# Finished head pairs normalised on GpSimd, a deeper evacuation queue and all-VectorE rungs in the last units

## The chip, the cores and the metric

The kernel runs on one core of a Trainium2 chip. The metric is the device time of one execution in microseconds. The engines named here are TensorE (PE in the profile, PEld for its weight loads), VectorE (DVE), ScalarE (ACT), GpSimd (POOL) and the DMA queues of SyncE (SP) and GpSimd. PSUM is the memory that TensorE writes its results to; SBUF is the working memory.

## The reference

Two attention layers over 2048 tokens, 512 channels and 32 heads of 16 channels run side by side, and their outputs are joined along the channels. Cut to what matters:

```
A (4 segments of 512 tokens, M and z carried from segment to segment):
  q, k, v = x@wq, x@wk, x@wv                 per head
  a_dot = softmax(q k^T * 16**-0.5, causal inside the segment) v
  a_mem = (phi(q) M) / (phi(q) z + 1e-6);  phi(t) = t+1 if t>0 else exp(t)
  o = g * a_mem + (1-g) * a_dot;           g = sigmoid(beta) per head
  M += phi(k)^T v ;  z += sum phi(k) ;     result  o @ wo
B (all 2048 tokens, no mask):
  o = softmax(q k^T * 16**-0.5) v ;        result  o @ wo
```

B's score matrices are the bulk: 32 heads of 2048 x 2048, each entry of which has to go through an exponential.

## The kernel before

**Units.** The work is cut into units. One unit holds four heads of one group of eight (the heads of one parity, `e`, of a row tile `rt`) for 512 queries. Two units, e = 0 and e = 1, make a pair. A has 16 pairs (four segments of four), B 16 pairs (four query blocks `ch` of four). The order is: A's four pairs of segment 0, then B and A pairs in turn until A's twelve others are used up, then B's last four pairs alone. A unit of B meets 16 key blocks of 128 keys; a pair of A is only five such blocks' worth, because of the mask.

**Two ways to exponentiate a key block.** On the first way, TensorE writes the scores of a key block (four heads, four banks of 512) into PSUM tiles `s_ps` of three and two banks in turn, and ScalarE exponentiates a tile at a time into `pT` (L906). For A, GpSimd then clears what the mask excludes (`affine_select`, L916). On the second way, which only B's key blocks can take, TensorE writes each head's scores into a one-bank tile `v_ps`, and VectorE turns them into 16-bit integers `vx` whose bits, read as float16, are an approximate exponential (L979, four evacuations a key block). Three more copies of that tile are made with other offsets from `LADDER`, so that the errors of the four average out. These copies are called rungs here. Two are made by VectorE (L993). The third is made in place by a DMA that adds a constant tile `fill` to `vx` once the first tile has been used (`v_sum`, L1000, issued from GpSimd's queue). All four are multiplied by the values, so a block on the second way costs TensorE four products with the values instead of one.

**Accumulators and pairs.** Products with the values go into a one-bank PSUM tile `acc` per unit. Three such one-bank slots exist, and `acc`, `v_ps`, the projections' results, A's memory products `am_ps` and the output projections all share them. When a unit is done, VectorE transposes `acc` into one half of an SBUF tile `tT` (L378, `fin_unit`). There is one `tT` only: `held["tT"]` is set when the first unit of a pair is transposed, and cleared when the pair is finished (`pair_end`). The next pair's first transpose has to wait for that. `fin_pair` (L396) then finishes the pair: a reciprocal of the softmax sums (L401), for A more small reciprocals, then the normalisation. For B and A's segment 0 that is one multiplication (L412); for A's later segments it is two multiplications and an addition (L420, L422, L424). Last comes a transpose into the output tile `OT` (L426). B's very last pair takes another way, `fin_half`.

**The planner.** The order of instructions on every engine is written out when the program is built, by a model of the engines' clocks (`T["pe"]`, `T["dve"]`, `T["pool"]` and so on). VectorE's work waits in a list of tasks and is put into the program when the model's VectorE gets to it; lower `prio` goes first, so evacuations (0) come before a pair's steps (1), and these before rungs (2). The first score tile of a key block for VectorE is issued only while `backlog()`, the model's VectorE work in hand, is below `VBACK` microseconds, and a one-bank slot is free (`v_scores`, L959). `v_pick` (L934) takes the key block: from the current unit or one of the next, at most three blocks ahead of the current unit, none when a unit has about three left (these go to ScalarE), and none before unit 8. So how many key blocks VectorE takes is not fixed; it follows from how early the model thinks VectorE is free.

**The way to GpSimd that is there already.** In `fin_pair` the normalising instructions ask for an engine by `yield (POOLTT, ...)`. `in_turn` (L741) gives GpSimd only if `T["pool"] < T["pe"] + POOLSLACK` and fewer than two such requests wait. With `POOLSLACK = -99` this is never so, and the instruction goes to VectorE. If it were so, `pool_run` (L1006) would hold the request until VectorE has at least `POOLWITH` = 1.2 microseconds of work queued that does not share SBUF's ports with GpSimd by the model (evacuations from PSUM; tasks marked `port` are the others), or until `POOLWAIT` = 4 microseconds have gone by. The model gives it `POOLTT` = 1.2 microseconds, and both sides keep clear of each other's `port` stretches (`clear`, `begin`, `on_pool`).

Of the kernel before, what the change touches and what calls it, by code (L numbers as in the profile page):

```python
# [37 lines left out]
LADDER = (12914, 13046, 13325, 13628)  # L38
# [1 line left out]
VBUFS = 12  # L40
VMIN = 3
VLATE = 0.5
VBACK = 1.0
BANKS = (3, 2)
PBUFS = 8
SWITCH = 0.095
# [12 lines left out]
DMARUNG = 3  # L59
# [4 lines left out]
SPLOADS = 38.0  # L64
SPTRANS = 1.5
POOLTT = 1.2
POOLSLACK = -99.0
POOLWITH = 1.2
POOLWAIT = 4.0
LEAD = 2.5  # L70
# [7 lines left out]
def kernel(  # L78
# [21 lines left out]
    def pin(ins):  # L100
        return tc.keep_in_program_order(ins)
# [42 lines left out]
    def later(us, f, src=None, prio=0, ready=None, ok=None, port=False):  # L144
        if not live[0]:
            f()
            return
        if ready is None:
            ready = T["pe"] + PELAT
        seq[0] += 1  # L150
        tasks.append(dict(prio=prio, seq=seq[0], ready=ready, us=us, f=f, src=src, ok=ok, port=port))
# [319 lines left out]
    with ExitStack() as ms:  # L471
# [51 lines left out]
        units, pos0, where = [], {}, 0.0  # L523
# [212 lines left out]
        def backlog():  # L736
            return max(0.0, T["dve"] - T["pe"]) + sum(t["us"] for t in runnable() if t["ready"] < T["pe"] + 0.6)
# [3 lines left out]
        def in_turn(g, prio, end=None):  # L741
            on = [None]

            def step():
# [7 lines left out]
                if isinstance(c, tuple):  # L752
                    if T["pool"] < T["pe"] + POOLSLACK and len(ptasks) < 2:
                        on[0] = nc.gpsimd
# [22 lines left out]
        def free_slots(at):  # L777
            return sum(s <= at for s in slots)
# [155 lines left out]
        def v_pick():  # L934
            if vnow[0] is not None:
                return True
            if vlive[0] > VBUFS - 2:
                return False
            vmin = VMIN + VLATE * (max(0.0, T["dve"] - T["pe"]) + sum(t["us"] for t in tasks)) / QUAD
            for i in range(u_at[0], min(u_at[0] + 5, len(units))):  # L940
                u = units[i]
                if u["name"] == "a" or len(u["kbs"]) < vmin:
                    continue
                kb = u["kbs"][-1]
                if i > cur[0] and vahead[0] >= VAHEAD or not has(u, kb) or i < VFROM:
                    return False
                u["kbs"].pop()
                u["left"] += len(LADDER)
                u["nv"] = u.get("nv", 0) + 1
                vlive[0] += 1  # L950
                vahead[0] += i > cur[0]
                x = wk.tile([P, 4, 512], U16, name="vx", tag="vx", bufs=VBUFS)
                vnow[0] = (u, kb, x, list(q4))
                return True
            return False
# [3 lines left out]
        def v_scores(taken, lim=2, force=False):  # L959

            n = 0
            while n < lim and (force or backlog() < VBACK) and free_slots(T["pe"] + (0.1 if taken else 0.0)) and v_pick():
                u, kb, x, left = vnow[0]
# [13 lines left out]
        def v_evac(u, kb, x, j, vt, end):  # L977
            def f():
                pin(nc.vector.tensor_scalar(x[:, j, :], vt[:], XSCALE, float(LADDER[0]), ALU.mult, ALU.add))  # L979
                if end:  # L980
                    buf = [len(LADDER) - 1, u, kb, x]
                    v_ready(u, kb, x, buf)
                    for i in range(1, len(LADDER)):
                        if i != DMARUNG:
                            later(0.70, v_rung(u, kb, x, LADDER[i], buf), prio=2, ready=T["dve"],
                                  ok=lambda: vlive[0] < VBUFS, port=True)
            return f

        def v_rung(u, kb, x, off, buf):
            def f():  # L990
                vlive[0] += 1
                p = wk.tile([P, 4, 512], U16, name="vx", tag="vx", bufs=VBUFS)
                pin(nc.vector.tensor_scalar(p[:], x[:], float(off - LADDER[0]), 32767.0, ALU.add, ALU.min))  # L993
                v_ready(u, kb, p, [1])
                v_done(buf)
            return f
# [22 lines left out]
        def v_ready(u, kb, p, buf, at=None):  # L1019
            pd = p[:].bitcast(F16)  # L1020
            pvq.append(dict(u=u, kb=kb, v=buf, ready=(T["dve"] + DVEEND if at is None else at) + 0.06,
                            parts=[(pd, j, j, (u, kb, 0, 512, 0), None) for j in q4]))
# [408 lines left out]
```

## Time and profile before

| what | value |
|---|---|
| median of three runs | 884.29 us (883.23 to 884.37) |
| the profiled execution's own time | 883.22 us |
| its span, first to last instruction | 881.5 us |
| busy: PE, ACT, DVE, POOL | 853.3, 854.8, 755.7, 269.6 us |
| ACT's exponentials, L906 | 736 instructions, 843.4 us |
| DVE's score evacuations, L979 | 528 (132 key blocks), 345.9 us |
| DVE's rungs, L993 | 264, 173.5 us |
| DMA rungs, L1000 | 132, 512 KB each, 4.9 us to landing |
| normalisations on DVE, L412, L420, L422, L424 | 19, 12, 12, 12 |
| granted TensorE clock | 0.998 |

A row of the table of groups gives the line, the engine and operation, the tile written and the tile read, shapes, the number of instructions, their busy time together, the mean of one in nanoseconds and, after the bar, the time for which the engine was idle just before them with what ended most of it. Instructions in a row on one engine overlap a little, so busy time over count is less than the mean. A stretch of the span, where one is shown, lists each engine's busy time in it. A time line gives the start, the duration, the engine and line, and in brackets the idle time before it.

### The profile page before, as it was taken

To read this page: it belongs to the slowest core of one execution; us is meant where nothing else is said; L and a number is where in the kernel's file an instruction comes from. 1 tells how busy PE (TensorE), PEld (TensorE's weight loads), DVE (VectorE), ACT (ScalarE), POOL (GpSimd) and SP (SyncE) were. 2 spreads that over 40 slices of the span, in tenths; PEclk is the share of its full clock that TensorE was granted. 3 is DMA by queue.
4 is the path that set the end of the run, shared out by engine and by line. 5 is a ranking of instruction groups with operands and counts; after the bars stand their busy time and mean duration, and the time that the engine had idled before them with its cause. 6 is when DMAs were issued, how large, how long until landed. Compare 5 with 4: busy or idle time off the path is not lost.

```text
span 881.5 us, 19327 instructions
## 1 busy us (share of the span) xinstructions
PE 853.3 (97%) x7725; PEld 253.6 (29%) x7725; DVE 755.7 (86%) x1280; ACT 854.8 (97%) x766; POOL 269.6 (31%) x466
## 2 busy tenths in 40 slices
PE   8999999999999999999999999999999999999995
PEld 3322222322323222222232223223232322222221
DVE  4778499889898888979989999888979899999994
ACT  6999999999999999999999999999999999999994
POOL 6711402433424134241331414215241411212111
PEclk9999999999999999999999999999999999999999
DMA  9404315345164554533547463554636355756754
GB/s 197 91 14 101 91 29 96 79 88 97 31 120 90 116 114 80 96 76 69 103 78 135 99 135 73 97 97 94 122 62 116 77 126 103 134 107 130 144 112 101
DMA packets 61811, 86.28 MB, mean 98 GB/s; under 512 B 36624, under 2 KB 44816, under 8 KB 61712
## 3 DMA queue, kind: packets, MB, share of 16 engines
q0 software_dynamic: 19008, 69.21, 41.7%
q1 hardware_dynamic: 41360, 15.23, 7.5%
q8 instruction: 62, 1.02, 0.5%
q10 hardware_dynamic: 1344, 0.52, 0.2%
q14 instruction: 37, 0.30, 0.1%
HBM read 4.20 MB, written 4.19 MB: 10 GB/s over the span
## 4 chain that ended last, share of the span: by engine, by line
PE 34%; ACT 15%; issue 7%; DVE 3%; DMA 1%; POOL 1%; ACTq 0%; POOLq 0%; DVEq 0%
PE acc L121 18%; ACT pT L906 15%; PE s_ps L121 9%; PE v_ps L121 5%; DVE vx L979 1%; DMA vx<-fill 1%; POOL pT L916 1%; DVE vx L993 1%; PE o_ps L121 1%; PE q_ps L121 0%; PE am_ps L121 0%; ACT ex L303 0%; DVE tT L378 0%; PE k_ps L121 0%; PE m_ps L121 0%
## 5 line engine op out<-in xcount | busy, mean ns | idle before, releaser
L906 ACT ACTIVATE pT<-s_ps 128x1536 bf16<-128x1536 f32 x736 | 843.4, 1284 | 8.6 <-PE s_ps L121 4.9
L979 DVE TENSOR_SCALAR vx<-v_ps 128x512 uint16<-128x512 f32 x528 | 345.9, 685 | 43.4 <-PE v_ps L121 34.4
L121 PE MATMUL s_ps<-qB,KB 32*128 32x512 bf16 x1520 | 245.3, 383 | 10.0 <-ACT pT L906 7.2
L1000 POOL DMA_DIRECT2D vx<-fill x132 | 115.9, 890 | 452.7 <-PE v_ps L121 132.2
L121 PE MATMUL v_ps<-qB,KB 32*128 32x512 bf16 x528 | 188.3, 381 | 1.0 <-DVE vx L979 0.5
L121 PE MATMUL acc<-vx,VB 128*32 128x512 f16 x2112 | 185.2, 384 | 2.8 <-DMA vx<-fill 1.1
L993 DVE TENSOR_SCALAR vx<-vx 128x2048 uint16<-128x2048 uint16 x264 | 173.5, 690 | 2.6
L121 PEld LDWEIGHTS <-KB 32*128 32x128 bf16 x2048 | 82.5, 91 | 249.5 <-issue 244.1
L121 PE MATMUL acc<-pT,VB 128*32 128x512 bf16 x1520 | 147.2, 386 | 0.0
L916 POOL TENSOR_SCALAR_AFFINE_SELECT pT<-pT 128x256 bf16<-128x256 bf16 (+2 forms) x242 | 102.6, 455 | 68.9 <-ACT pT L906 67.9
L121 PE MATMUL acc<-zeros 128*128 128x512 bf16 x369 | 123.3, 386 | 0.0
L121 PEld LDWEIGHTS <-VB 128*32 128x32 bf16 x3632 | 74.6, 94 | 164.7 <-issue 149.6
L121 PE MATMUL s_ps<-qA,kA 32*128 32x512 bf16 (+3 forms) x512 | 53.1, 300 | 2.8 <-ACT pT L906 1.5
L378 DVE STREAM_TRANSPOSE tT<-acc 128x512 f32<-128x512 f32 x64 | 44.5, 700 | 12.7 <-PE acc L121 12.7
L121 PEld LDWEIGHTS <-zeros 128*128 128x128 bf16 x385 | 31.0, 97 | 71.6 <-issue 64.8
L278 POOL TENSOR_SCALAR qA<-qc,par 128x512 bf16<-128x512 bf16 x24 | 18.4, 775 | 59.9 <-DVE qc L276 59.9
L121 PE MATMUL acc<-pT,vA 128*32 128x256 bf16 (+3 forms) x512 | 31.6, 305 | 1.2 <-DVE vA L323 0.5
L276 DVE CAST qc<-q_ps 128x512 bf16<-128x512 f32 x28 | 19.2, 685 | 10.4 <-PE q_ps L121 9.6
L121 PEld LDWEIGHTS <-kA 32*128 32x128 bf16 x512 | 16.9, 92 | 38.4 <-issue 36.1
L278 POOL TENSOR_SCALAR qB<-qc,par 128x512 bf16<-128x512 bf16 x32 | 23.3, 746 | 9.4 <-DVE qc L276 9.4
L458 DVE CAST osb<-o_ps 128x512 bf16<-128x512 f32 x28 | 19.2, 687 | 6.7 <-PE o_ps L121 6.7
L121 PE MATMUL o_ps<-wo_a,OT_a 128*128 128x512 bf16 x64 | 19.8, 384 | 0.0
(93 smaller groups left out, 432.2 us busy)
## 6 DMA issues: line engine op xcount, KB each, us to landing
vx<-fill POOLq DMA_DIRECT2D x132, 512.0 KB, 4.9
out_dram<-osb SPq DMA_DIRECT2D x30, 128.0 KB, 1.7
w_b<-in_B_wqkv_dram SPq DMA_DIRECT2D x3, 512.0 KB, 5.8
phk<-phkT SPq DMA_TRANSPOSE x48, 2.4
w_a<-in_A_wv_dram SPq DMA_DIRECT2D x1, 512.0 KB, 4.3
wo_a<-in_A_wo_dram SPq DMA_DIRECT2D x1, 512.0 KB, 4.7
wo_b<-in_B_wo_dram SPq DMA_DIRECT2D x1, 512.0 KB, 8.1
xT_b<-in_B_x_dram SPq DMA_TRANSPOSE x28, 2.9
```

The source lines that it names most:

```text
L121: return pin(nc.tensor.matmul(out, lhsT, rhs, **k))
L276: pin(nc.vector.tensor_copy(qc[:], ps[:]))
L278: pin(nc.gpsimd.tensor_scalar(dst[:, e, :], qc[:], par[:, e:e + 1], 0.0, ALU.mult, ALU.add))
L378: pin(nc.vector.transpose(st["tT"][:, e].rearrange("p c d -> p (c d)"), acc[:]))
L458: pin(nc.vector.tensor_copy(osb[:], ps[:]))
L906: pin(nc.scalar.activation(pT[:, 0:n, :], pt[:, 0:n, :], ACT.Exp, scale=SCALE))
L916: pin(nc.gpsimd.affine_select(out=blk, in_=blk, compare_op=ALU.is_ge, fill=0.0, base=0, pattern=[[0, len(sls)], [1, P]], channel_multiplie ...
L979: pin(nc.vector.tensor_scalar(x[:, j, :], vt[:], XSCALE, float(LADDER[0]), ALU.mult, ALU.add))
L993: pin(nc.vector.tensor_scalar(p[:], x[:], float(off - LADDER[0]), 32767.0, ALU.add, ALU.min))
L1000: pin(nc.gpsimd.dma_start(out=x[:].rearrange("p j c -> p (j c)").rearrange("p (a c) -> p a c", c=FILL), in_=fill[:].to_broadcast([P, 2048 ...
```

## The change

Three things are changed, all in what the planner decides.

1. `POOLSLACK` goes from -99 to 1.0. The normalising multiplications and additions of finished pairs may now go to GpSimd, under the conditions given above. Whether each one does depends on the model at that moment.
2. `VBACK` goes from 1.0 to 1.5. Score tiles for VectorE are issued while the model has up to 1.5 microseconds of VectorE work in hand.
3. In the last two units (B's last pair) the third rung is no longer made by the DMA: `buf` gets the count of all four rungs and no tile for `v_sum`, and the loop makes one more `v_rung` task, a VectorE pass of L993's kind into a buffer of its own.

```diff
-VBACK = 1.0
+VBACK = 1.5
...
-POOLSLACK = -99.0
+POOLSLACK = 1.0
...
                 if end:
                     buf = [len(LADDER) - 1, u, kb, x]
+                    if u["id"] >= len(units) - 2:
+                        buf = [len(LADDER)]
                     v_ready(u, kb, x, buf)
                     for i in range(1, len(LADDER)):
-                        if i != DMARUNG:
+                        if i != DMARUNG or u["id"] >= len(units) - 2:
                             later(0.70, v_rung(u, kb, x, LADDER[i], buf), prio=2, ready=T["dve"],
                                   ok=lambda: vlive[0] < VBUFS, port=True)
```

## The prediction

> **What bounds the kernel now.** I read the page's busy times and groups first, then three stretches of the span, then VectorE's own waits, then two pieces of the time line: a hand-over between pairs and the end. From the table of groups:
>
> ```profile
> L906 ACT ACTIVATE pT<-s_ps 128x1536 bf16<-128x1536 f32 x736 | 843.4, 1284 | 8.6 <-PE s_ps L121 4.9
> L979 DVE TENSOR_SCALAR vx<-v_ps 128x512 uint16<-128x512 f32 x528 | 345.9, 685 | 43.4 <-PE v_ps L121 34.4
> L1000 POOL DMA_DIRECT2D vx<-fill x132 | 115.9, 890 | 452.7 <-PE v_ps L121 132.2
> L121 PE MATMUL acc<-zeros 128*128 128x512 bf16 x369 | 123.3, 386 | 0.0
> L993 DVE TENSOR_SCALAR vx<-vx 128x2048 uint16<-128x2048 uint16 x264 | 173.5, 690 | 2.6
> ```
>
> And the stretches with A mixed in, and with B alone (us, then busy time of PE, PEld, DVE, ACT, POOL):
>
> ```profile
> 45.00:705.00 660.00, 646.21 (x5830) 191.72 (x5832) 573.71 (x975) 654.57 (x588) 204.39 (x343) 1.00 0.46 89
> 705.00:865.00 160.00, 157.06 (x1511) 45.04 (x1503) 150.88 (x248) 158.67 (x140) 31.36 (x36) 1.00 0.64 123
> ```
>
> ScalarE is busy for 99% of both, and its exponentials wait 8.6 us in all. It is the bound. TensorE looks as full, but 369 of its matrix products multiply zeros into an accumulator: filler that gives way. So the time is ScalarE's count of key blocks, and it falls only if VectorE takes more of them. VectorE idles 660 - 573.7 = 86 us in the mixed stretch, 9 us in B's own.
>
> **The exchange rate.** A key block is four banks of L906's 1840 (736 tiles of 2.5): 4 x 843.4/1840 = 1.83 us of ScalarE. On VectorE it is 4 x 345.9/528 + 2 x 173.5/264 = 2.62 + 1.31 = 3.93 us. A block that moves shortens the span by 1.83 us, and VectorE, kept at its present share of 0.86, loses 0.86 x 1.83 = 1.57 us of room. It therefore takes 5.50 us of VectorE time to move one block, and a freed microsecond of VectorE is worth 1.83/5.50 = one third of a microsecond. TensorE pays three more groups of products a block, 0.22 us apart in the time line of the end: 0.65 us, out of the filler's 123 us.
>
> **Part 1, normalisation on GpSimd.** The rows, each shape apart:
>
> ```profile
> L412 DVE TENSOR_TENSOR tN<-tT,rsum 128x512 bf16<-128x512 f32 x15 | 10.5, 703 | 0.1
> L424 DVE TENSOR_TENSOR tN<-tT,aT 128x512 bf16<-128x512 f32 x12 | 8.6, 715 | 0.4
> L422 DVE TENSOR_TENSOR aT<-aT,r 128x512 f32<-128x512 f32 x12 | 8.2, 680 | 0.0
> L420 DVE TENSOR_TENSOR tT<-tT,r 128x512 f32<-128x512 f32 x12 | 7.7, 646 | 0.0
> L278 POOL TENSOR_SCALAR qB<-qc,par 128x512 bf16<-128x512 bf16 x32 | 23.3, 746 | 9.4 <-DVE qc L276 9.4
> ```
>
> That is 35.0 us in 51 instructions. (The four of A's segment 0 come before VectorE takes key blocks, and free nothing.) GpSimd is 31% busy in the mixed stretch, and a request that meets it busy stays on VectorE; I take 47 of 51, 32 us, worth 10.7 us of span. Bounds 28 to 35 us.
>
> What it costs: GpSimd's instruction has no row. The nearest is L278 with one input, 0.68 us alone and up to 1.64 us behind VectorE; I take 1.3 us, bounds 0.7 and 2.4 (L278's mean alone, and that mean on top of its longest). The Trainium skill, GPSIMD Engine Reference, section 4.1 Engine selection, speaks against the move: two-input elementwise work belongs on VectorE, and GpSimd is about twice as slow. By it the instruction would take about 1.4 us, an estimate, and the sum would be the same to 0.2 us.
>
> Queued behind it on GpSimd are mask clears (L916), query splits (L278) and DMA issues (L1000). A delay of 1.3 us there I cost at nothing: the eight `pT` tiles between ScalarE and the products last 8 x 1.15 = 9.2 us. If that cover went, ScalarE would wait for each microsecond beyond it. The output projections behind L426 have due times eight tiles and more later, so SP's stores move with no cost.
>
> Now the wait. The request may be held for up to 4 us, and L426, `held["tT"]` and the next pair's first transpose stand behind it. The time line of VectorE at a hand-over from B to A:
>
> ```profile
> 220.52 0.71 DVE L378 STREAM_TRANSPOSE tT<-acc 128x512 f32<-128x512 f32 x1
> ...
> 225.64 0.68 DVE L412 TENSOR_TENSOR tN<-tT,rsum 128x512 bf16<-128x512 f32 x1
> 226.36 0.71 DVE L426 STREAM_TRANSPOSE OT_b<-tN 128x512 bf16<-128x512 bf16 x1
> 226.99 0.68 DVE L378 STREAM_TRANSPOSE tT<-acc 128x512 f32<-128x512 f32 x1
> ```
>
> A's first transpose starts as soon as B's pair lets go of `tT`: so at 8 of the 12 such hand-overs (the other four have 0.8 to 2.9 us between). Each microsecond of delay keeps one of three PSUM slots from score tiles. I take 2.0 us of holding and 0.6 us of slower instruction at the eight and 1 us at the four: 25 us, of which VectorE loses half, since a third slot and rungs are left to it: 12 us, worth -4.0. Bounds 0 and 12 x (4.0 + 0.5) = 54 us. After A's pairs nothing presses: the next transpose comes 12 to 21 us later.
>
> **Contention.** VectorE and GpSimd hold each other up when both work from SBUF (GpSimd's two query splits, then VectorE's two-input instruction):
>
> ```profile
> 336.05 2.31 POOL L278 TENSOR_SCALAR qB<-qc,par 128x512 bf16<-128x512 bf16 x2 [0.91 <-DVE qc L276]
> ```
>
> ```profile
> 336.25 1.03 DVE L309 SCALAR_TENSOR_TENSOR phq<-ex,po 128x512 bf16<-128x512 f32 x1
> ```
>
> L309 takes 0.69 us undisturbed. L979 beside GpSimd work keeps its 0.685. The worst stretch of a rung is 0.24 us (0.93 against 0.69). I take 0.1 us for each of 47, 4 us rounded, worth -1.3; bounds 0 and 47 x 0.7 = 33 us, a rung that waits out half an instruction each time. The Trainium skill, SBUF — State Buffer, section Who interferes with whom, calls the shared port an exclusive lock: the later one waits for the whole instruction, which the stretched rows here only show in part. By it, if every instruction met a rung, the estimate is 47 x 1.3 = 61 us, -20 instead of -1.3.
>
> **Part 2, the deeper queue.** VectorE's waits:
>
> ```profile
> DVE vx L979 <- PE v_ps L121: 34.4, 91, 1.4
> DVE vx L979 <- PE s_ps L121: 4.1, 12, 0.9
> ```
>
> A mean gap of 0.38 us before an evacuation would be covered by 0.5 us more in hand, if a slot is free, which with three it often is not. Some gaps come from the limit of three blocks ahead, which stays. Bounds 0 and 38 us; I take 15, worth 5.0. The wait it adds is before projections' evacuations in the same queue, 0.5 us at most, again under the 9.2 us of `pT`.
>
> **Part 3, the end.** Time line, all engines:
>
> ```profile
> 865.95 0.86 POOL L1000 DMA_DIRECT2D vx<-fill  x1 [3.08 <-PE acc L121]
> ...
> 869.03 0.39 PE L121 MATMUL acc<-vx,VB 128*32 128x512 f16 x4
> 870.51 0.40 PE L121 MATMUL acc<-vx,VB 128*32 128x512 f16 x4 [1.09 <-DMA vx<-fill]
> ...
> 870.96 0.72 DVE L378 STREAM_TRANSPOSE tT<-acc 128x512 f32<-128x512 f32 x1 [5.54 <-PE acc L121]
> ```
>
> Without the DMA the last product ends at about 869.5, as its neighbours do: 1.4 us gained directly (bounds 0 and 1.5); late next are ScalarE's last tile (its products start at 868.60) and the fixed end after it. The last two units hold ten blocks for VectorE (11 of 16 on ScalarE in each): ten passes of 0.657 us, 6.6 us, of which 1.3 lies in the 5.5 idle us above. 5 us, worth -1.7. Ten DMA issues of 0.88 us leave GpSimd, where nothing waits for them.
>
> **Sum.** 10.7 - 4.0 - 1.3 + 5.0 - 1.7 + 1.4 = 10.1 us off the profiled execution's 883.22 (span 881.5 and 1.7 around it): 873.1. That execution is 1.1 us under the median, so 874.2, rounded to 874.0.
>
> **Rivals.**
> - *The hold at the hand-over eats it* (slower). One mechanism: at the 12 B-to-A hand-overs one slot is left, so 1.2 us of evacuations cannot be queued, the request runs into its 4 us, and all of it is lost. 54 us, -18 instead of -4: 884.3 + 18 - 14.1 = 888. It decides from 4.0 us lost at each (48 us, -16). For it: the eight tight hand-overs; against: rungs, which need no slot.
> - *GpSimd's instruction takes 2.4 us where the plan has 1.2* (slower). VectorE's queue stands at L426 behind it: 51 x 1.2 = 61 us, -20: about 894. For it: two inputs, float, strided; against: L278's 0.68.
> - *Freed time is not taken up*: the three-ahead limit and the slots hold the blocks at 132. Then only the end is left, 884.3 - 1.4 = 883, up to 880. For it: idle time in A's pairs is there already; against: B's own stretch, with VectorE at 94%.
> - *Both gains whole*: 35 us and 30 us, no lost hand-over: 11.7 + 10 - 1.3 - 1.7 + 1.4 = 20 us: 864.
>
> **How the numbers follow.** Forecast 0.48; hold 0.17; long instruction 0.08; not taken up 0.13 (half of it within 0.2% of before); both whole 0.14. 0.2% (1.8 us) is about what a measurement of this kernel tells from no change; the runs spread over 1.1 us. Faster 0.48 + 0.14 + 0.06 = 0.68, same 0.07, slower 0.25. The range: 861 is the best of all bounds but the queue's (11.7 + 11.7 - 1.7 + 1.4 = 23); 889 takes in the hold and leaves out the long instruction. The forecast's own range is 866 to 880.
>
> **What the profile after would show.** Right: L412 to L424 on POOL, some 47; L979 x548 or so, L906 near 728; DVE's wait for v_ps under 25 us; L378 after L426 at hand-overs some 2 us later than before; at the end no DMA wait before the last product, and ten L1000 fewer, less those that come with new blocks. Wrong: L979 still x528 (not taken up); DVE idle before L426 with POOL named (long instruction); DVE idle before L378 or fewer L979 in A's pairs (hold).

## The result, and the profile after

The changed kernel takes 885.19 us (883.35 to 886.48 in four runs) against 884.12 us before: a ratio of 1.0012, 95% interval 0.9993 to 1.0032. It made no difference that can be measured. I had forecast 874.0, with 861 to 889 as the range and 0.07 for "same". The profiled execution is the longest of the four, 886.48 us with a span of 884.8; its sums below go against the 883.22 and 881.5 of before. It had a granted clock of 0.994; the fastest of the four had 0.998, as before, and took 883.35.

The costliest groups of the changed kernel, the same five as were shown of before (L1002 and L995 are the old L1000 and L993):

```profile
L906 ACT ACTIVATE pT<-s_ps 128x1536 bf16<-128x1536 f32 x728 | 836.5, 1275 | 18.5 <-PE s_ps L121 11.4
L979 DVE TENSOR_SCALAR vx<-v_ps 128x512 uint16<-128x512 f32 x548 | 358.6, 684 | 40.8 <-PE v_ps L121 36.3
L1002 POOL DMA_DIRECT2D vx<-fill x128 | 117.9, 924 | 368.4 <-PE acc L121 95.9
L995 DVE TENSOR_SCALAR vx<-vx 128x2048 uint16<-128x2048 uint16 x283 | 197.2, 718 | 1.7
L121 PE MATMUL acc<-zeros 128*128 128x512 bf16 x326 | 113.1, 387 | 0.0
```

VectorE did take more: 548/4 = 137 key blocks instead of 132, and ScalarE ran 8 tiles fewer, 836.5 us instead of 843.4. The gain was made and then given back. ScalarE's idle time is the span less its busy time: 881.5 - 854.8 = 26.7 us before, 884.8 - 849.0 = 35.8 after, 9.1 more, against 5.8 us less of work in all. Before L906 alone it grew from 8.6 to 18.5 us. The mean rung went from 690 to 718 ns. The stretches with A mixed in and with B alone show where:

```profile
45.00:705.00 660.00, 632.74 (x5771) 188.99 (x5821) 578.48 (x974) 644.21 (x576) 242.95 (x373) 0.99 0.48 93
705.00:865.00 160.00, 156.16 (x1501) 44.72 (x1504) 149.88 (x249) 158.60 (x140) 34.73 (x40) 1.00 0.51 100
```

ScalarE lost 10.4 us of its 654.6 in the mixed stretch, where most of the pairs are finished, and nothing in B's own. For the first time the granted clock (the column after the five engines) is below 1.00 there.

The normalisations on GpSimd, from its groups with each shape apart:

```profile
L420 POOL TENSOR_TENSOR tT<-tT,r 128x512 f32<-128x512 f32 x12 | 13.8, 1147 | 15.2 <-DVE r L407 10.0 <-DVE r L416 5.2
L422 POOL TENSOR_TENSOR aT<-aT,r 128x512 f32<-128x512 f32 x11 | 13.2, 1201 | 2.5 <-DVE r L417 2.5
L424 POOL TENSOR_TENSOR tN<-tT,aT 128x512 bf16<-128x512 f32 x7 | 10.6, 1511 | 1.6 <-DVE aT L422 1.4
L412 POOL TENSOR_TENSOR tN<-tT,rsum 128x512 bf16<-128x512 f32 x4 | 4.5, 1114 | 9.1 <-DVE rsum L401 9.0
```

These are 34, and one of A's segment 0 besides. What they do to VectorE is seen at one pair of A, first VectorE's time line, then GpSimd's:

```profile
447.62 0.35 DVE L417 RECIPROCAL r<-r 128x32 f32<-128x32 f32 x1
447.89 3.25 DVE L995 TENSOR_SCALAR vx<-vx 128x2048 uint16<-128x2048 uint16 x2
```

```profile
447.59 1.38 POOL L420 TENSOR_TENSOR tT<-tT,r 128x512 f32<-128x512 f32 x1
448.61 1.36 POOL L422 TENSOR_TENSOR aT<-aT,r 128x512 f32<-128x512 f32 x1
```

Two rungs take 3.25 us where two take 1.3. The first alone is 2.64 us long in the trace: it ends at 450.53, 0.56 us after the second of GpSimd's instructions. Of the 283 rungs 16 met a normalisation; 11 of these took 0.80 to 2.64 us, and they make 8.5 of the 9.0 us that all rungs together take above 686 ns each. The way from a late rung to ScalarE, in the time line of all engines at another pair:

```profile
346.53 2.76 DVE L995 TENSOR_SCALAR vx<-vx 128x2048 uint16<-128x2048 uint16 x2
346.57 1.56 POOL L424 TENSOR_TENSOR tN<-tT,aT 128x512 bf16<-128x512 f32 x1
...
348.74 0.40 PE L121 MATMUL acc<-vx,VB 128*32 128x512 f16 x4 [0.69 <-DVE vx L995]
...
349.68 0.39 PE L121 MATMUL s_ps<-qB,KB 32*128 32x512 bf16 x3
...
350.17 1.45 ACT L906 ACTIVATE pT<-s_ps 128x1536 bf16<-128x1536 f32 x1 [0.86 <-PE s_ps L121]
```

The rung is late; TensorE's queue, whose products start in the order written, stands 0.69 us at the rung's product; the score tile queued behind it is late; ScalarE, the bound, waits 0.86 us.

Twice before the end the granted clock also fell to half, at 249.6 and at 512.5 us, for 3.4 us each time. Ahead of both it was another VectorE pass from SBUF to SBUF that met a normalisation: L308 took 1.16 and 1.53 us, where none takes over 0.43 in e5_thin below. Ahead of the first, the rung behind it was late without being stretched, and TensorE stood at its product:

```profile
245.46 1.27 POOL L424 TENSOR_TENSOR tN<-tT,aT 128x512 bf16<-128x512 f32 x1
245.72 1.16 DVE L308 TENSOR_SCALAR po<-qc 128x512 bf16<-128x512 bf16 x1
...
248.33 0.62 PE L121 MATMUL acc<-vx,VB 128*32 128x512 f16 x8 [0.86 <-DVE vx L995]
```

The stretches around this drop (us, busy times, granted clock after POOL's):

```profile
246.20:249.60 3.40, 2.54 (x25) 0.75 (x24) 3.30 (x6) 2.98 (x3) 1.15 (x2) 1.00 0.02 5
249.60:253.10 3.50, 3.18 (x21) 0.98 (x21) 2.94 (x7) 2.48 (x2) 1.53 (x3) 0.51 0.48 91
253.10:256.50 3.40, 3.37 (x22) 0.93 (x23) 2.75 (x6) 2.88 (x3) 0.00 (x0) 1.00 0.32 60
```

That these waits brought the drops is read from their places, and from e5_thin, where the stretched passes and the drops are gone together.

The end went as forecast. No DMA stands before the last product; ScalarE's last tile ends at 872.77 + 1.05 = 873.82, and 10.98 us are left of the span, where before it was 881.5 - 868.65 = 12.85:

```profile
872.77 1.05 ACT L906 ACTIVATE pT<-s_ps 128x1024 bf16<-128x1024 f32 x1
...
873.39 0.87 PE L121 MATMUL acc<-pT,VB 128*32 128x512 bf16 x8
...
874.30 0.72 DVE L378 STREAM_TRANSPOSE tT<-acc 128x512 f32<-128x512 f32 x1 [4.83 <-PE acc L121]
```

### The profile page after: what moved, and what is told of

Its sections match the earlier page's. It is cut to its first block, busy times and chain, and to the rows that moved or that the text cites. A ratio compares the mean times of both kernels' runs of the same rounds, so it can differ in the third digit from the quotient of the medians.

```text
span 884.8 us, 19287 instructions
## 1 busy us (share of the span) xinstructions
PE 841.9 (95%) x7682; PEld 251.3 (28%) x7742; DVE 763.7 (86%) x1284; ACT 849.0 (96%) x758; POOL 310.0 (35%) x498
## 5 line engine op out<-in xcount | busy, mean ns | idle before, releaser
L906 ACT ACTIVATE pT<-s_ps 128x1536 bf16<-128x1536 f32 x728 | 836.5, 1275 | 18.5 <-PE s_ps L121 11.4
L979 DVE TENSOR_SCALAR vx<-v_ps 128x512 uint16<-128x512 f32 x548 | 358.6, 684 | 40.8 <-PE v_ps L121 36.3
L121 PE MATMUL s_ps<-qB,KB 32*128 32x512 bf16 x1500 | 242.0, 384 | 12.0 <-ACT pT L906 7.2
L1002 POOL DMA_DIRECT2D vx<-fill x128 | 117.9, 924 | 368.4 <-PE acc L121 95.9
L121 PE MATMUL acc<-vx,VB 128*32 128x512 f16 x2192 | 193.6, 385 | 6.3 <-DVE vx L995 2.7
L995 DVE TENSOR_SCALAR vx<-vx 128x2048 uint16<-128x2048 uint16 x283 | 197.2, 718 | 1.7
L121 PE MATMUL v_ps<-qB,KB 32*128 32x512 bf16 x548 | 192.6, 382 | 3.0 <-DVE KB L257 0.7
L121 PEld LDWEIGHTS <-VB 128*32 128x32 bf16 x3692 | 76.9, 94 | 172.0 <-issue 154.3
L121 PE MATMUL acc<-zeros 128*128 128x512 bf16 x326 | 113.1, 387 | 0.0
L121 PEld LDWEIGHTS <-zeros 128*128 128x128 bf16 x342 | 28.1, 97 | 71.5 <-issue 67.2
L420 POOL TENSOR_TENSOR tT<-tT,r 128x512 f32<-128x512 f32 x12 | 13.8, 1147 | 15.2 <-DVE r L407 10.0
```

Source lines behind the costliest of these rows:

```text
L121: return pin(nc.tensor.matmul(out, lhsT, rhs, **k))
L420: pin(eng.tensor_tensor(t1, t1, rr.to_broadcast(bc), op=ALU.mult))
L906: pin(nc.scalar.activation(pT[:, 0:n, :], pt[:, 0:n, :], ACT.Exp, scale=SCALE))
L1002: pin(nc.gpsimd.dma_start(out=x[:].rearrange("p j c -> p (j c)").rearrange("p (a c) -> p a c", c=FILL), in_=fill[:].to_broadcast([P, 2048 ...
```

## The experiments

The theory after this look: GpSimd's normalisations collide with VectorE's passes from SBUF to SBUF, and the late passes starve ScalarE by way of TensorE's queue. The rivals: the hold at the hand-over, the deeper queue, and the clock. Each measurement is given as the median and then the ratio of the means, with its interval, against runs of before on the same chip. Where two kernels are compared below, each is taken against its own before.

### The same order of work with thin instructions on GpSimd (e5_thin)

```diff
+            n = 1 if eng is nc.gpsimd else 16
-            pin(eng.tensor_tensor(t1, t1, rr.to_broadcast(bc), op=ALU.mult))
+            pin(eng.tensor_tensor(t1[:, :, 0:n], t1[:, :, 0:n], rr[:, :, 0:n].to_broadcast([P, 2, n, DH]), op=ALU.mult))
...
```

The other three are cut in the same way, and `tN` is one tile throughout, cleared once. So the kernel leaves out most of the normalisation of the pairs on GpSimd.

> The changed kernel with the same order of work on every engine, but each normalising instruction on GpSimd touches 32 of 512 columns only (so most of a normalised pair is left undone); its long hold of SBUF's ports is gone, the hold at the hand-over is not. Theory (collisions: VectorE's rungs and other passes that meet GpSimd's normalisations are stretched, TensorE's queue stands behind the late products, ScalarE starves and the clock drops): the rung's mean falls from 718 to about 690 ns, ScalarE's idle time after the start falls from 18.6 to about 9 us, no drop of the clock, time 875 to 877. Rival (the hold at the hand-over and the deeper queue delay score tiles): nothing changes, 883 to 886. Rival (noise of the clock alone): 883.

Measured: 875.62 us, ratio 0.9913 (0.9900 to 0.9926). The rung (now L1001) is back, the clock is whole between 10 and 860 us, and ScalarE waits for score tiles half as long:

```profile
L1001 DVE TENSOR_SCALAR vx<-vx 128x2048 uint16<-128x2048 uint16 x283 | 188.4, 686 | 1.7
```

```profile
ACT pT L912 <- PE s_ps L121: 6.3, 11, 1.8
```

This is what the theory expected. VectorE, ScalarE and GpSimd run the instructions of the changed kernel in the same order (but for that one clearing), on the same 137 key blocks, and 9.1 us disappear when GpSimd's are thin: 8.0 under its before, where the changed kernel is 1.1 over. The hold and the deeper queue are unchanged in it, so they don't make the loss.

### Thin instructions, four in a row (e9_thin4)

The edit, against e5_thin:

```diff
+            for _ in range(4 if eng is nc.gpsimd else 1):
-            pin(eng.tensor_tensor(t1[:, :, 0:n], ...
+                pin(eng.tensor_tensor(t1[:, :, 0:n], ...
```

> The thin kernel (e5_thin, 875.6 us) with each thin instruction on GpSimd issued four times: 4 x 0.24 us, so GpSimd is occupied about as long as by the whole instruction, and a pair is let go as late, but SBUF's ports are held in short pieces (most of a normalised pair is left undone, as there). If the long hold of the ports is what costs: rung's mean 690 to 700 ns, 876 to 879. If it is GpSimd's time as such (late release at the hand-over, mask clears and DMA issues behind it): 883 to 886, the changed kernel's time, without longer rungs.

Measured: 876.52 us, ratio 0.9918 (0.9905 to 0.9932). GpSimd's 140 instructions sum to 48 us in the trace, more than the 43 us of the changed kernel's 35, and the rung's mean is 691 ns. The median is 0.9 us above e5_thin's, and the two intervals overlap: GpSimd's time as such, with the later release of `tT` and whatever queues behind it, makes little of the 9 us. Rungs that meet thin instructions are hardly touched: 31 did, and none took over 0.86 us. One of them (VectorE's time line, then GpSimd's):

```profile
344.02 1.38 DVE L1005 TENSOR_SCALAR vx<-vx 128x2048 uint16<-128x2048 uint16 x2
```

```profile
344.27 2.21 POOL L432 TENSOR_TENSOR tN<-tT,aT 128x32 bf16<-128x32 f32 x4
```

### Every instruction on GpSimd twice (e8_twice)

```diff
+            for _ in range(2 if eng is nc.gpsimd else 1):
-            pin(eng.tensor_tensor(t1, t1, rr.to_broadcast(bc), op=ALU.mult))
+                pin(eng.tensor_tensor(t1, t1, rr.to_broadcast(bc), op=ALU.mult))
...
```

> The changed kernel with each of its 35 instructions on GpSimd issued twice (so some pairs are normalised wrongly) and the same order of work otherwise. Theory (collisions): twice the port time, rung's mean 740 to 760 ns, 10 us or more on top of the changed kernel, 895 to 905. Rival (the hold at the hand-over): the second instruction adds 1.2 us at each, no rung is longer, 888 to 892.

Measured: 918.69 us, ratio 1.0389 (1.0345 to 1.0433), worse than either expectation.

```profile
L999 DVE TENSOR_SCALAR vx<-vx 128x2048 uint16<-128x2048 uint16 x283 | 211.5, 768 | 1.7
```

The rung's mean is 768 ns and ScalarE waits 33.2 us for `s_ps`. Doubling the load costs 34 us more where the first load cost 9.1; the granted clock falls to 0.971 over the profiled span. That late waits bring further ones is how I read this; what the waits and the clock each take was not separated.

### The whole normalisation in four and in eight pieces (e12_four, e13_eight)

```diff
+    def pieces(eng):
+        n = 4 if eng is nc.gpsimd else 16
+        return [(a, a + n) for a in range(0, 16, n)]
...
+            for a, b in pieces(eng):
+                pin(eng.tensor_tensor(t1[:, :, a:b], t1[:, :, a:b], rr[:, :, a:b].to_broadcast([P, 2, b - a, DH]), op=ALU.mult))
...
```

In e13_eight the 4 is a 2.

> The changed kernel with the same order of work, the whole normalisation done, but each instruction on GpSimd cut into four along its 16 blocks (140 instead of 35). If it is the length of one hold of SBUF's ports that costs: rungs wait for a piece (0.3 to 0.5 us) instead of the whole, rung's mean 695 to 702 ns, 877 to 880, better than both kernels. If it is the total time for which GpSimd holds the ports: rungs are stretched as before or more (over 718 ns), 884 to 889.

> The same in eight pieces (280 instructions of about 0.27 us, together 2.1 us for one instruction of 1.1). If the length of one hold costs: as e12_four or 1 us better, 876 to 880. If the total time costs, or GpSimd's delay behind it: 886 to 892.

Measured: 888.32 us, 1.0051 (1.0032 to 1.0070), and 894.65 us, 1.0131 (1.0103 to 1.0159). The first is what the second answer expected, the second lies 3 us beyond either. But most rungs do get in between two pieces: of 31 that met them in e12_four all but three took 0.95 us or less, and of 37 in e13_eight all but two 0.86 or less. The few others stand through many pieces (1.96 to 3.54 us, 4.34 and 5.19 us) and make 6.0 of the 9.6 us and 8.2 of the 10.9 us of stretch. The longest stands through the last two pieces of one instruction and all of the next two (VectorE's time line, then GpSimd's):

```profile
660.46 5.19 DVE L1003 TENSOR_SCALAR vx<-vx 128x2048 uint16<-128x2048 uint16 x1
```

```profile
658.79 2.16 POOL L426 TENSOR_TENSOR tT<-tT,r 128x64 f32<-128x64 f32 x8
660.82 2.11 POOL L429 TENSOR_TENSOR aT<-aT,r 128x64 f32<-128x64 f32 x8
662.84 2.25 POOL L432 TENSOR_TENSOR tN<-tT,aT 128x64 bf16<-128x64 f32 x8
```

So the rungs are stretched as much in all as by whole instructions (720 and 725 ns in the mean, against 718), and cutting doesn't help. What decides whether a rung gets in or stands, no run here settles. Nor is the rest of the loss taken apart: the pieces take longer in all (69 and 94 us of GpSimd, against 43), and the granted clock differs; the one run of e12_four at 0.996 takes 884.31, no more than the changed kernel at that clock (885.0 and 885.38).

### One part at a time (e1_pool, e2_queue, e3_last)

```diff
-POOLSLACK = -99.0
+POOLSLACK = 1.0
```

> Before with POOLSLACK 1.0 alone: 36 normalisations on GpSimd, three key blocks more on VectorE (135). Theory (collisions): three blocks are 5.5 us less of ScalarE and stretched passes cost about as much or more, 883 to 887, rung's mean over 700 ns. Rival (the deeper queue does the harm): 879, the three blocks show in full.

Measured: 885.60 us, 1.0027 (1.0017 to 1.0037); 135 key blocks, rung's mean 711 ns. Three blocks more and still slower: as the theory says. One of its two clock drops before the end, at 338.1 us, begins in a wait of another kind: GpSimd issued a DMA rung at 331.94, after seven mask clears in a row, and TensorE stood 2.50 us at its product:

```profile
339.30 0.62 PE L121 MATMUL acc<-vx,VB 128*32 128x512 f16 x4 [2.50 <-DMA vx<-fill]
```

```diff
-VBACK = 1.0
+VBACK = 1.5
```

> Before with VBACK 1.5 alone: 133 key blocks on VectorE, one more. Theory (collisions): no normalisation on GpSimd, so no stretch, rung's mean 690 ns, 882 to 883. Rival (the deeper queue does the harm): 885 or more, ScalarE's idle time up by 3 us or more without any stretched rung.

Measured: 890.00 us, 1.0077 (1.0061 to 1.0093). Here my theory's number is wrong and the rival's comes true: the rung's mean is 686 ns, ScalarE idles 7.5 us more than before, and the deeper queue alone is the slowest of the three parts. TensorE's time line and the stretches around it say why:

```profile
213.64 0.58 PE L121 MATMUL k_ps<-xT_a,w_a 128*128 128x512 bf16 x1 [2.64 <-DMA xT_a<-in_A_x_dram]
```

```profile
200.00:213.30 13.30, 10.88 (x108) 3.66 (x101) 10.96 (x23) 11.40 (x10) 3.98 (x5) 1.00 0.97 132
213.30:223.50 10.20, 9.86 (x54) 1.52 (x53) 5.26 (x8) 5.71 (x5) 0.86 (x1) 0.50 0.47 90
```

With another plan, one projection of A stands in TensorE's queue 2.6 us ahead of its transposed input. The clock then halves for 10 us, and ScalarE is busy for 5.71 of the 10.20 us: 4.5 us lost there. Its wait before the tile at 214.87 is 3.2 us, half of it ahead of the drop.

```diff
                     if end:
                         buf = [len(LADDER) - 1, u, kb, x]
+                        if u["id"] >= len(units) - 2:
+                            buf = [len(LADDER)]
...
-                        if i != DMARUNG:
+                        if i != DMARUNG or u["id"] >= len(units) - 2:
```

> Before with the last units' passes alone: 131 key blocks, one fewer (+1.8 us of ScalarE), and the end after ScalarE's last tile 1.9 us shorter. Both theories: 883 to 885, no difference that can be told from none.

Measured: 883.31 us, 0.9994 (0.9985 to 1.0003), as expected: one block fewer and a shorter end cancel.

### The queue and the end without GpSimd (e4_queue_last, e7_load, e11_deeper)

e4_queue_last is the changed kernel with `POOLSLACK = -99.0`.

> The changed kernel with POOLSLACK back at -99: deeper queue and the last units' passes, 133 key blocks. Theory (collisions): one block is 1.8 us, the end is about 1.9 us shorter, 880 to 881, no stretched rungs. Rival (the deeper queue does the harm): 884 or more.

Measured: 883.63 us, 1.0026 (1.0002 to 1.0049), not the theory's 880 to 881, with the same wait for `xT_a` (2.64 us) in its profile. Its eleven runs go with the clock: six with a granted clock of 0.997 or 0.998 take 882.8 to 883.6 us, five with 0.987 to 0.995 take 887.5 to 894.2. e7_load takes that wait away by letting the planner count on the loads later:

```diff
-                rel = T["sp"] + 4.0
+                rel = T["sp"] + 7.0
...
-                            c["after"] = T["sp"] + 4.0
+                            c["after"] = T["sp"] + 7.0
...
```

The same is done for B's x and the output weights.

> The queue with the last units' passes and no normalisation on GpSimd (e4_queue_last), but the planner counts on x's transposed loads 7 us after their issue instead of 4, so that no projection is put into TensorE's queue ahead of its data; 134 key blocks, two more than before. Theory (the deeper queue is harmless by itself, one 2.6 us wait for xT_a and the half clock after it ate the gain): no wait over 1 us on TensorE between 20 and 860 us, no drop of the clock there, 134 blocks are 3.7 us less of ScalarE and the end is 1.9 us shorter: 878 to 880. Rival (a deeper queue delays score tiles in general): 883 or more with the clock whole.

Measured: 880.73 us, 0.9967 (0.9954 to 0.9980), all five runs within 1 us, 0.7 us above the theory's range and faster than both kernels. Its exponentials wait 10.6 us in all, and no wait on TensorE between 20 and 860 us reaches 1 us:

```profile
L906 ACT ACTIVATE pT<-s_ps 128x1536 bf16<-128x1536 f32 (+1 forms) x733 | 839.3, 1282 | 10.6 <-PE v_ps L121 4.7 <-PE s_ps L121 4.2
```

So in this plan depth 1.5 does no harm by itself. e11_deeper goes on from there:

```diff
-VBACK = 1.5
+VBACK = 2.0
```

> No normalisation on GpSimd, the last units' passes, loads after 7 us (as e7_load, 880.7 us) and VBACK 2.0: 136 key blocks, two more. If depth is harmless: 877 to 879, no stretched rungs. If a deeper queue delays score tiles: 882 or more, with ScalarE waiting for s_ps.

Measured: 883.82 us, 1.0003 (0.9994 to 1.0012). The time is the rival's, its sign is not: ScalarE waits 4.5 us for `s_ps`, 4.2 in e7_load. The kernel has its two blocks more, and an accident of its own, TensorE's wait for a DMA rung, near the end of which the clock halves for 3.4 us:

```profile
337.79 0.62 PE L121 MATMUL acc<-vx,VB 128*32 128x512 f16 x4 [4.70 <-DMA vx<-fill]
```

GpSimd had issued that DMA at 332.54, after nine mask clears in a row. Its rungs are stretched too, though no normalisation is on GpSimd: 695 ns in the mean, one of them 1.96 us beside mask clears. Whether depth 2.0 makes such waits likelier, or this plan only had bad luck, one plan can't tell.

### More filler for the clock (e6_warm)

```diff
-WARMTH = 0.52
+WARMTH = 0.60
```

> The changed kernel with the planner's floor of TensorE activity at 0.60 instead of 0.52: 472 zero products instead of 326, 139 key blocks. If the drops of the clock make the loss: none of them between 10 and 860 us, 874 to 878. If the stretched rungs and the waits behind them make it, and the clock only adds: stretched rungs stay (mean 710 to 720 ns), 879 to 884.

Measured: 894.97 us, 1.0130 (1.0112 to 1.0148), outside both expectations. One drop of the clock instead of two, 139 key blocks, and 28 rungs that met GpSimd instead of 16, mean 728 ns. The drops alone don't make the loss: the run with a granted clock of 0.997 still takes 892.5 us. More filler ahead of score tiles (472 zero products) does not cure it either. How much of the extra 10 us the filler and the stretched rungs each bring was not taken apart.

### One instruction a pair on GpSimd (e10_one)

```diff
-            eng = (yield (POOLTT, 0.7)) or nc.vector
-            pin(eng.tensor_tensor(t2, t2, r2[:].to_broadcast(bc), op=ALU.mult))
+            yield -0.7
+            pin(nc.vector.tensor_tensor(t2, t2, r2[:].to_broadcast(bc), op=ALU.mult))
...
```

L424 is treated likewise, and the loads are counted on after 7 us as in e7_load.

> The changed kernel with one instruction a pair allowed on GpSimd instead of three for A's later segments (17 go there instead of 35), and the planner counting on x's transposed loads after 7 us instead of 4; 137 key blocks as in the changed kernel. Theory (collisions): half the instructions, half the stretched rungs (mean about 700 ns), 877 to 881, one drop of the clock at most. Rival (any use of GpSimd for pairs costs as much as it frees): 883 to 886.

Measured: 880.85 us, 0.9968 (0.9955 to 0.9980). Faster than before, and no better than e7_load, which leaves GpSimd alone. The time is in the theory's range, but its sign is missed: with half the instructions the rung's mean is still 715 ns, not about 700. Nine rungs that met normalisations make 5.9 of the 8.3 us of stretch; most of the rest is beside mask clears, one rung alone 2.35 us long.

## Why the prediction was wrong

- **The bound and the exchange rate: right.** ScalarE bounds both kernels. Five blocks and the shorter end should be worth 5 x 1.83 + 1.4 = 10.6 us; e5_thin, which has them without the collisions, is 8.0 us under its before. Where the other 2.6 went was not traced; its exponentials wait 9.8 us, against 8.6.
- **How many blocks move: right in sum, by luck.** I had net room for 26/5.50 = 4.7 blocks; five moved, from other parts. GpSimd took 34 of the 51 instructions, not 47, which freed 4 x 0.70 + 12 x 0.65 + 11 x 0.68 + 7 x 0.72 = 23 us, not 32. By the plans, the parts give three blocks (normalisation), one (queue) and minus one (end); all three at once give five.
- **GpSimd's instruction: right.** 1.11 to 1.51 us by row, taken as 1.3. The Trainium skill's factor of about two (GPSIMD Engine Reference, section 4.1 Engine selection) roughly holds: 1.15 against 0.65 us for L420, 1.51 against 0.72 for L424, and 1.6 to 2.1 over the four rows.
- **Contention: this step failed.** I took 4 us of VectorE's time "worth -1.3" (47 x 0.1 is 4.7, worth -1.6; the slip is small). It cost 9.1 us, the difference between the changed kernel and e5_thin, or 8.4 against e9_thin4. About 2 of these go with the clock: the changed kernel's run at 0.998 is 1.8 us under its median. It was wrong twice. The size: 283 rungs at 718 instead of 686 ns are 9.1 us, and L308 adds 2.9. And the rate: one third of a microsecond holds for time that the planner knows of and answers with fewer blocks. Time that VectorE loses on the chip against the plan isn't answered. It makes one product late, and with it everything behind it in TensorE's queue, ScalarE's tiles among them. In the changed kernel the loss reached the bound nearly one for one. That rate is not fixed: e10_one, with 8.3 us of stretched rungs, loses 5.0 us against e5_thin, in a plan with later loads. I had both rows in hand (L309 at 1.03 us, a rung at 0.93) and read them as averages. The rule that I weighed there, the exclusive lock of the Trainium skill, SBUF — State Buffer, section Who interferes with whom, was closer than my term: 2.64 us for a rung behind two instructions is a full block, and more than "for the whole instruction", since the second instruction began after the rung. But not every instruction met a rung, as the 61 us there supposed: 16 rungs met one.
- **The deeper queue: over-sized, and with a cost that I gave as nothing.** 15 us of VectorE were to come, nearly three blocks; by the plan the queue alone brings one (e2_queue). And a new plan moves projections against their loads: 2.64 us of TensorE and half a clock for 10 us in e2_queue. I had looked at which evacuations wait, not at which DMA the moved step needs. In the changed kernel as a whole that wait doesn't occur.
- **The end: right.** 12.85 us from ScalarE's last tile to the end became 10.98, and e3_last is no different from before.
- **The hold at the hand-over** (-4.0, and as a rival 888): not the loss, and over-sized. I counted twelve hand-overs from B to A. By the trace GpSimd took the multiplication at one of them, at 226 us; its three others for B are in B's own stretch, where the next transpose comes 14 to 16 us later. e5_thin and e9_thin4 keep it and are 0.8 to 0.9% faster than before. What it costs by itself was not measured.
- **The rivals.** "Freed time is not taken up" comes near the time (883) with the wrong cause: five blocks were taken up. "Both gains whole" missed by 21 us. "GpSimd's instruction takes 2.4 us" is refuted by the rows. No rival had the collision as its mechanism, though a term of the sum named it. The range's lower end takes 11.7 (35 us) for the queue, a figure without a row, where the bound above it was 38 us; nothing rests on it.

## What to carry to other kernels

Where an order of work is written out ahead from a model, price lost time by whom it surprises: a microsecond that the model knows of is shared out, one that it doesn't know of stands in front of the bound and can take the clock along. Before work goes to GpSimd, look for VectorE passes from SBUF to SBUF near it: evacuations from PSUM bore it without loss (683 to 685 ns in every run), rungs and L308 did not. And when a knob changes a written-out order, look in the new trace for single waits of TensorE over a microsecond before judging the knob: one of 2.6 us hid the gain of the deeper queue, and without it the deeper queue and the new end gave 0.33%, with no normalisation on GpSimd at all.

## What the runs showed of the hardware

- A rung that meets GpSimd's normalisations can stand until several of them in a row are done: 2.64 us behind two, 5.19 us behind pieces of 64 columns that kept coming. Most rungs that met pieces of 64 or 128 columns got in between them, at 0.95 us or less, and runs of 32-column instructions let two rungs through in 1.38 us. Mask clears in a row can hold a rung up as well (2.35 us in e10_one). The 29 evacuations from PSUM that met a normalisation in the changed kernel took 0.69 us at most.
- In the changed kernel the granted clock fell to half after stretches in which TensorE was busy only in part: 2.54 of 3.40 us ahead of the drop at 249.6 us, most of it in products of 32 columns or rows, and came back after 3.4 us there, after 10.2 us in e2_queue. The Trainium skill, TensorE: Matmul & The Clock Gate, section What's actually happening, has the clock halve after an idle window of about 3.4 us; the length of the drops agrees, but in the changed kernel a window that was busy for three quarters by the profile was enough.
- One program can differ by 11 us from run to run, in step with its granted clock: e4_queue_last took 882.8 us at 0.997 and 894.2 us at 0.987.
